# When the short block's first scores are computed, and where the gathers stand in a place

## The chip, the cores and the metric

The kernel runs on one core of a Trainium2 chip. The metric is the device time of one execution in microseconds (us). It is one program: an attention stage, and behind it a feed-forward stage. The change touches the attention stage alone.

## What is computed

Talking-heads attention over 8 images of 12 heads, 448 tokens and 64 channels, and then a feed-forward layer on its result:

```python
scores = scale * np.matmul(q, k.transpose(0, 1, 3, 2))
scores = np.einsum('bhij,hg->bgij', scores, w_pre)
scores = scores - np.max(scores, axis=-1, keepdims=True)
attn = np.exp(scores)
attn = attn / (np.sum(attn, axis=-1, keepdims=True) + 1e-09)
attn = np.einsum('bhij,hg->bgij', attn, w_post)
out = np.matmul(attn, v)
x = out.transpose(0, 2, 1, 3).reshape(B * S, H * D)
h = x @ w_in
y = (h - np.tanh(h)) @ w_out
```

## The kernel before

**Blocks, groups and places.** The 448 query tokens of an image `b` are cut into four chunks `m`: 120, 120, 120 and 88 tokens. A block is one chunk of one image (32 blocks, `i` = 4b + m); the short block is the one with m = 3. Heads are mixed with the 10 tokens x 12 heads of a group on the partitions, so each block is 12 groups (9 for the short one), 360 in all. Two groups are worked on together, in one pass of the main loop, which is called a place here; there are 180 places `p`, some 22 or 23 per image.

**What every place does.** TensorE (PE) multiplies the gathered scores of its two groups by `w_pre` (`premix`, L920). VectorE (DVE) takes the row maxima (`mx`, L929), ScalarE (ACT) the exponentials (L931), GpSimd (POOL) folds the sums into `w_post` (`norm`, `wr`, L940), and PE multiplies by that (`mix`, L957), for the place before. ACT copies the result to `at` at the start of the next place (L967).

**What some places do besides.** Each block also needs: its q transposed (`prep_q`, L842, from `qr`, loaded by `load_q`), its scores (`scores`, six head pairs, L876, copied out of PSUM by ACT and DVE in L881 to the tile `s`), and its values (`values`, two halves, L1000, copied by DVE in L1018). Each image also needs its keys transposed (`prep_k`, L816, copied to `kk` by L827 and L828). These jobs are dealt out to places by a planner ahead of the loop: `halved` lists for each job its earliest and its latest place, and the loop behind it gives each place the waiting job with the nearest latest place, one of the other kind (scores, `"s"`, or values, `"v"`) where that is possible. `prep_q` is put one place ahead of the first scores of its block, the `load_q` of the next block on the place of these scores, and `prep_k` where there is room. Two further planner steps spread single pairs over empty places. Every engine runs its instructions in the order in which they are written.

**Buffers around the change.** The scores of a block lie in `s` (tile pool `sp`, two buffers), token by token; `gather` (L909) is a DMA that moves the rows of one group from `s` to a tile `t` with the heads next to the tokens. So block i+1 writes where the last gathers of block i-1 read. In place p the two gathers for place p + 3 are issued. `ps_m` is a pool of four PSUM banks: a score pair takes two, a `prep_q`, `prep_k` or half of the values takes one each.

**SyncE's queue (SP).** All DMAs of this stage go through SyncE's queue, in order. Gathers are put there at once by `gather`. All other DMAs (loads of q, k and v, stores of `x`, and the DMAs of the weight conversion) are put on two lists, `queue` and `slow`, and `issue(6)` sends up to six of them in each place, those that were put there in an earlier place.

**The weight conversion.** In the background `Convert` splits the weights of the feed-forward layer in two parts and writes these and sums of them to DRAM (`cr` in, `wi`, `wo`, `ss`, `ts` out). `conv.step()` emits one phase of it per place on DVE (L81 and L82 in one phase, L90, L91 and L94 in another), ACT (L86, L99) and POOL (L84 to L129); `conv.more()` puts further loads on the list `slow`.

Of the kernel before, what the change touches and what calls it, by code (L numbers as in the profile page):

```python
# [148 lines left out]
def kernel_body(  # L149
# [74 lines left out]
    def open_early():  # L224
        ff.hid = pool("hid", 1, "left")
        ff.bias = pool("bias", 1, "left").tile([P, 2 * LINE], F32, name="bias", tag="bias")
        nc.gpsimd.memset(ff.bias[:, 0:1], GATE_A[1])
        nc.gpsimd.memset(ff.bias[:, 1:2], GATE_B[1])
        nc.gpsimd.memset(ff.bias[:, 2:3], -0.25)
        ff.xr, ff.xe, ff.xqa = pool("xr", 1, "left"), pool("xe", 1, "left"), pool("xqa", 1, "left")  # L230
        ff.plain = ctx.enter_context(ExitStack())
        ff.w0, ff.xp = pool("w0", 3, "left", ff.plain), pool("xp", NK, "left", ff.plain)

    def open_ps_h():
        ff.ps_h = ctx.enter_context(tc.tile_pool(name="ps_h", bufs=2, space=PSUM, side="left"))
# [501 lines left out]
    with ExitStack() as st:  # L737
# [32 lines left out]
        def issue(most):  # L770
            for x in (queue, slow):
                while x and most and x[0][0] < place[0]:
                    send(x, nc.sync)
                    most -= 1
# [131 lines left out]
        def gather(t, eng=nc.sync):  # L906
            i, g = groups[t]
            x = tq[t % RT]
            eng.dma_start(x[D - HP : D - HP + rows[t], :], sts[i][tokens[t].start : tokens[t].stop : tokens[t].step])  # L909
            tg[t] = x  # L910

        def premix(p):


            pss = [ps_p.tile([P, S], F32, name="ps_p", tag="ps_p") for _ in halves]
            ts = [tg.pop(2 * p + j) for j in range(2)]
            for j in (1, 0):
                for r in (1, 0):
                    k = slice(r * D, D + r * H * half_rows(2 * p + j)[r])
                    nc.tensor.matmul(pss[r][halves[j], :], wpre[k, :], ts[j][k, :], start=True, stop=True)  # L920
            return pss

        def expo(p, pss):
            zs = gp.tile([P, 3, 2], F32, name="zs", tag="zs")
            es = []
            for r, ps in enumerate(pss):

                mx = gp.tile([P, 1], F32, name="mx", tag="mx")
                nc.vector.tensor_reduce(out=mx, in_=ps, axis=AX.X, op=ALU.max, negate=True)  # L929
                e = gp.tile([P, S], F32, name="e", tag="e", bufs=4)  # L930
                nc.scalar.activation(e, ps, AF.Exp, bias=mx, scale=1.0, accum_out=zs[:, 0, r : r + 1])  # L931
                es.append(e)
            te[p] = [es, zs]

        def norm(p):
            zs = te[p][1]
            wr = gp.tile([P, 2, D], F32, name="wr", tag="wr", bufs=2)[:, :, :HP]
            nc.vector.tensor_scalar_add(zs[:, 1], zs[:, 0], 1e-9)
            nc.vector.reciprocal(zs[:, 2], zs[:, 1])  # L939
            nc.gpsimd.tensor_mul(  # L940
                wr, wpost[:, :HP].unsqueeze(1).to_broadcast([P, 2, HP]), zs[:, 2].unsqueeze(2).to_broadcast([P, 2, HP])
            )
            te[p].append(wr)

        def mix(p):

            es, _, wr = te.pop(p)
            ps = ps_o.tile([P, 2, 512], F32, name="ps_o", tag="ps_o")
            for j in range(2):
                i, g = groups[2 * p + j]  # L950
                if g == 0:
                    ats[i] = kp.tile([CP, NC, H, MT], F32, name="at", tag="at", bufs=2)
            for r, e in enumerate(es):
                for c in range(NC):
                    for j, a in enumerate(halves):
                        k = slice(a.start, a.start + H * half_rows(2 * p + j)[r])
                        nc.tensor.matmul(  # L957
                            ps[:CP, j, c * GP : (c + 1) * GP].rearrange("p (h i) -> p h i", i=GI)[:, :, r * GH : (r + 1) * GH],
                            e[k, c * CP : (c + 1) * CP], wr[k, r, :],
                            start=True, stop=True,  # L960
                        )

            def rest():
                (i0, _), (i1, _) = groups[2 * p], groups[2 * p + 1]
                n0, n1, at = rows[2 * p] // H, rows[2 * p + 1] // H, at_of[2 * p]
                if i0 == i1 and n0 == n1 == GI:
                    nc.scalar.copy(  # L967
                        ats[i0][:, :, :, at : at + 2 * GI].rearrange("p c h (j i) -> p j (c h) i", j=2),
                        ps[:CP, :, : NC * GP].rearrange("p j (x i) -> p j x i", i=GI),
                    )  # L970
                    return
                for j, (i, n) in enumerate(((i0, n0), (i1, n1))):
                    at = at_of[2 * p + j]
                    nc.scalar.copy(
                        ats[i][:, :, :, at : at + n],
                        ps[:CP, j, : NC * GP].rearrange("p (c h i) -> p c h i", c=NC, i=GI)[:, :, :, :n],
                    )

            return rest
# [102 lines left out]
        for w in range(2):  # L1082
            for at in AT[w]:
                x = repeat[:, w, at : at + HP].rearrange("p (i h) -> p i h", i=GH)
# [7 lines left out]
        for w in range(2):  # L1092
            for a in range(2):
                if w == 0:
                    x = both[:, w, a].rearrange("p (i g) -> p i g", i=GH)
                    of, step = ps_w[:, w, :].unsqueeze(1).to_broadcast([P, GH, H]), [[H, GH], [0, H]]
                else:
                    x = both[:, w, a].rearrange("p (g i) -> p g i", i=GH)
# [38 lines left out]
        NG = len(groups)  # L1137
# [16 lines left out]
        halved = []  # L1154
        for i in range(len(blocks)):

            f0, f1, f2 = first[i : i + 3]
            if i + 1 < len(blocks):
                lo = max(0, (f0 - 1) // 2 - 2)
                hi = f1 // 2 - 4  # L1160
                for x in range(0 if i else 1, 3):
                    e = lo + 2 * x if lo + 4 <= hi else lo + (hi - lo) * x // 2
                    halved.append((e if i else x - 1, hi, "s", i + 1, x))
            for x in range(2):
                halved.append(((f1 - 1) // 2 + 2, f2 // 2 + 1 if f2 < NG else NPL + 7, "v", i, x))
        at_s, at_v, p, kind = {}, {}, 0, None
        window = {i: (lo, hi) for lo, hi, k, i, _ in sorted(halved, reverse=True) if k == "s"}
        while halved:
            ready = sorted((x for x in halved if x[0] <= p), key=lambda x: (x[1], x[3:]))
            if ready:  # L1170
                x = ready[0]
# [3 lines left out]
                if x[2] == kind and other and x[1] > p + 1:  # L1175
                    x = other[0]
                halved.remove(x)
                _, _, kind, i, n = x
# [11 lines left out]
        def held(p):  # L1190
            return [a for f, *a in todo[p] if f is scores]

        for p in range(1, NPL):
            if any(f in (scores, values) for f, *a in todo[p]):
                continue
            for of, n in ((p - 1, 1), (p + 1, 0)):
                if len(held(of)) == 2 and window[held(of)[n][0]][0] <= p <= window[held(of)[n][0]][1]:
                    i, hp = held(of)[n]
# [4 lines left out]
        for i, (b, m) in enumerate(blocks):  # L1203
            p0 = first[i] // 2
            if i + 2 < len(blocks):
                p = at_s[i + 2, 0] - 1
# [8 lines left out]
        for b in range(1, B):  # L1215
            p, o, done = first[blocks.index((b - 1, 1))] // 2 - 5, 0, []
            for hq in range(3):
                if hq == 2:

                    p = max(p, done[0] + 1)  # L1220
# [41 lines left out]
        for p in range(NPL + 3):  # L1262
            if mixed:
                mixed()
                mixed = None
            if 2 <= p < NPL + 1:
                if p not in short:
                    conv.step()
                conv.more()
            place[0] += 1  # L1270
            for t in range(2 * p + 6 if p else 4, 2 * p + 8):
                if t < NG:
                    gather(t)
            issue(6)
            if p == NPL + 1:
                for f in start.pop(p):
                    f()
            if p < NPL:
                ps = premix(p)
            if 1 <= p < NPL + 1:  # L1280
                norm(p - 1)
            if p == NPL:
                for f in x0[1:]:
                    f()
            if p < NPL:
                expo(p, ps)
            if p > NPL:
                next(xq)
                next(xq)
            for f, *a in todo[p]:  # L1290
                f(*a)
            for f in sooner:
                f()
            sooner.clear()
            if 1 <= p < NPL + 1:
                mixed = mix(p - 1)
            for f in then + last:
                f()
            then.clear()
            last.clear()  # L1300
            if p == NPL - 3:
                conv.rest(now)
                early.close()
                open_early()
            if p == NPL - 1:
                early_ps.close()
                open_ps_h()
            for f in start.get(p, ()):
                f()
            for _ in range(pieces.get(p, 0)):  # L1310
                next(xl)
# [20 lines left out]
    late, left = None, 4 * NQ  # L1332
    for s in range(NS):
        more = s + 1 < NS
        for p in range(NQ):
# [16 lines left out]
            late = pair_step(s, p, late, share, between)  # L1352
# [16 lines left out]
        late = None  # L1369
# [33 lines left out]
```

## Time and profile before

| what | us |
|---|---|
| median of 3 timed runs | 1688.39 |
| their lowest and highest | 1685.31, 1690.20 |
| the profiled execution's own time | 1691.88 |
| its span, from the first to the last instruction | 1690.2 |
| PE busy | 1654.1 |
| DVE busy | 1235.9 |
| ACT busy | 1090.9 |
| POOL busy | 613.9 |

The profile shows one execution. Its lines name an engine, a line of the kernel, and what is written and read (`s<-ps_q` writes `s` from `ps_q`). In the lines of a timeline the first number is the start in the span, the second the duration, xN the number of instructions merged in the row, and the brackets at the end hold the engine's idle time just before and what ended it. In the lines by stretch come the stretch, its length, each engine's busy time in it (PE, weight loads, DVE, ACT, POOL) with the number of instructions, the granted share of PE's clock, the share of the DMA engines that was busy, and GB/s. The attention stage's places run from 25.92 us to some 834 us of the span.

### The profile page before, as it was taken

The page shows a single profiled execution, that of the slowest core. Times are in us where ns is not written, and L with a number is a line of the kernel's source. Part 1 is how long each engine was busy: PE and PEld are TensorE (multiplying, and loading weights), DVE is VectorE, ACT ScalarE, POOL GpSimd, SP SyncE. Part 2 cuts the span into 40 slices and gives each one's busy share as a digit, 9 for nine tenths or more (in the row PEclk, how much of TensorE's full clock was granted, in tenths as well). Part 3 has the DMA queues.
Part 4 walks back from the last instruction along what each step waited for, and adds up shares of the span by engine and source line. Part 5 has one row for each costly group of instructions (what it writes and reads, how often), then busy time and mean ns, then how long its engine had stood idle before and what let it go on. Part 6 is the DMA issues. An engine that isn't in the chain of part 4 may idle for free.

```text
span 1690.2 us, 40990 instructions
## 1 busy us (share of the span) xinstructions
PE 1654.1 (98%) x16068; PEld 1380.8 (82%) x16068; DVE 1235.9 (73%) x1939; ACT 1090.9 (65%) x1896; POOL 613.9 (36%) x824
## 2 busy tenths in 40 slices
PE   8999999999999999999999999999999999999999
PEld 6777777777777777777788888888888888889999
DVE  5777786877867777776497999868778868778422
ACT  4777776677767677776576776556667356666331
POOL 2577666767666677664100111201111101012100
PEclk9999999999999999999999999999999999999999
DMA  9878788798978979875778899989999989988993
GB/s 191 232 249 239 248 245 253 236 269 256 260 229 260 257 246 261 263 238 201 229 248 321 286 324 319 346 288 343 330 324 358 358 272 338 325 321 321 412 413 134
DMA packets 322672, 475.08 MB, mean 281 GB/s; under 512 B 105648, under 2 KB 255664, under 8 KB 322480
## 3 DMA queue, kind: packets, MB, share of 16 engines
q1 hardware_dynamic: 305660, 414.34, 76.7%
q0 software_dynamic: 16512, 57.68, 8.6%
q8 instruction: 128, 2.10, 0.5%
q14 instruction: 64, 0.52, 0.1%
q10 hardware_dynamic: 308, 0.43, 0.1%
HBM read 274.73 MB, written 120.59 MB: 234 GB/s over the span
## 4 chain that ended last, share of the span: by engine, by line
PE 84%; DVE 6%; DMA 4%; ACT 3%; issue 2%; POOL 1%; SPq 0%; DVEq 0%; ACTq 0%; POOLq 0%
PE ps_o L957 14%; PE ps_m L1000 8%; PE ps_p L920 8%; PE ps_h L289 7%; PE ps_h L292 7%; PE ps_h L290 7%; PE y L532 6%; PE ps_q L876 6%; PE y L530 6%; PE y L531 6%; PE ps_m L842 1%; DMA w<-wo 1%; DMA t<-s 1%; PE ps_m L816 1%; DVE mx L929 1%
## 5 line engine op out<-in xcount | busy, mean ns | idle before, releaser
L957 PEld LDWEIGHTS ps_o<-wr,e 60*112 60x112 f32 (+1 forms) x5760 | 304.0, 175 | 32.7 <-POOL wr L940 17.2
L957 PE MATMUL ps_o<-wr,e 60*112 60x60 f32 (+1 forms) x5760 | 313.0, 258 | 7.0 <-POOL wr L940 5.7
L931 ACT ACTIVATE e<-ps_p,mx 128x448 f32<-128x448 f32 x360 | 225.4, 632 | 110.9 <-DVE mx L929 55.8
L929 DVE TENSOR_REDUCE mx<-ps_p 128x1 f32<-128x448 f32 x360 | 206.6, 616 | 78.6 <-PE ps_p L920 78.1
L967 ACT COPY at<-ps_o 112x960 f32<-112x960 f32 x156 | 153.9, 987 | 104.1 <-PE ps_o L957 103.7
L920 PE MATMUL ps_p<-t,wpre 60*64 60x448 f32 (+1 forms) x1440 | 179.1, 565 | 1.6 <-DMA t<-s 1.6
L940 POOL TENSOR_TENSOR wr<-wpost,zs 128x120 f32<-128x120 f32 x180 | 69.9, 388 | 265.6 <-DVE zs L939 204.8
L1000 PEld LDWEIGHTS ps_m<-at,vr 112*64 112x64 f32 x3072 | 151.2, 139 | 18.5 <-issue 12.9
L1000 PE MATMUL ps_m<-at,vr 112*64 112x120 f32 (+1 forms) x3072 | 164.8, 265 | 0.0
L530 PE MATMUL y<-w,gh 128*128 128x384 f32 x440 | 148.4, 337 | 4.1 <-DMA w<-wo 3.0
L531 PE MATMUL y<-w,gh 128*128 128x384 f32 x440 | 147.6, 336 | 0.0
L532 PE MATMUL y<-w,gl 128*128 128x384 f32 x416 | 140.4, 337 | 2.5 <-DVE gl L448 2.5
L881 DVE COPY s<-ps_q 120x448 f32<-120x448 f32 (+1 forms) x192 | 112.3, 615 | 24.6 <-DMA t<-s 12.5
L876 PEld LDWEIGHTS ps_q<-kk,qh 64*120 64x120 f32 (+1 forms) x768 | 58.6, 173 | 85.2 <-issue 44.6
L876 PE MATMUL ps_q<-kk,qh 64*120 64x448 f32 (+1 forms) x768 | 121.6, 393 | 1.2 <-DVE kk L828 0.5
L881 ACT COPY s<-ps_q 120x448 f32<-120x448 f32 (+1 forms) x192 | 94.8, 535 | 19.9 <-DMA t<-s 9.6
L305 ACT ACTIVATE u<-h 128x1024 f32<-128x1024 f32 x56 | 59.6, 1064 | 72.0 <-DVE h L717 68.1
L645 POOL DMA_DIRECT2D gs<-ga x24 | 17.5, 730 | 242.5 <-DVE ga L328 242.5
L530 PEld LDWEIGHTS y<-w,gh 128*128 128x128 f32 x440 | 82.6, 188 | 9.0 <-issue 4.7
L531 PEld LDWEIGHTS y<-w,gh 128*128 128x128 f32 x440 | 82.6, 188 | 3.3
L442 ACT CAST gh<-gl 128x1024 fp32r<-128x1024 f32 x60 | 62.5, 1041 | 28.7 <-DMA gl<-gs 18.0
L532 PEld LDWEIGHTS y<-w,gl 128*128 128x128 f32 x416 | 78.0, 188 | 3.4 <-DVE gl L448 3.4
(372 smaller groups left out, 3955.6 us busy)
## 6 DMA issues: line engine op xcount, KB each, us to landing
t<-s SPq DMA_DIRECT2D x342, 210.0 KB
wa<-ss SPq DMA_DIRECT2D x96, 384.0 KB
gl<-gs SPq DMA_DIRECT2D x62, 512.0 KB
w<-wo SPq DMA_DIRECT2D x41, 768.0 KB
wa<-wi SPq DMA_DIRECT2D x72, 384.0 KB
w<-ts SPq DMA_DIRECT2D x36, 768.0 KB
gs<-gs POOLq DMA_DIRECT2D x24, 768.0 KB, 8.5
cr<-in_moe_w_in_dram SPq DMA_DIRECT2D x48, 256.0 KB
```

The source lines that it names most:

```text
L289: nc.tensor.matmul(ph, w[:, c, 0], xh, start=start and c == 0, stop=False, skip_group_check=True)
L530: nc.tensor.matmul(y, gh[:, tok], wh, start=first, stop=False, skip_group_check=True)
L531: nc.tensor.matmul(y, gh[:, tok], wl, start=False, stop=False, skip_group_check=True)
L532: nc.tensor.matmul(y, gl[:, tok], wh, start=False, stop=last, skip_group_check=True)
L876: nc.tensor.matmul(ps[:n, :S], qx[a, hp, :], kx[a, hp % 2], start=(x == 0), stop=(x == 2))
L881: eng(sts[i][:n, 2 * hp + j, :], ps[:n, :S])
L920: nc.tensor.matmul(pss[r][halves[j], :], wpre[k, :], ts[j][k, :], start=True, stop=True)
L929: nc.vector.tensor_reduce(out=mx, in_=ps, axis=AX.X, op=ALU.max, negate=True)
L931: nc.scalar.activation(e, ps, AF.Exp, bias=mx, scale=1.0, accum_out=zs[:, 0, r : r + 1])
L957: nc.tensor.matmul(ps[:CP, j, c * GP : (c + 1) * GP].rearrange("p (h i) -> p h i", i=GI)[:, :, r * GH : (r + 1) * GH], e[k, c * CP : (c + ...
L967: nc.scalar.copy(ats[i0][:, :, :, at : at + 2 * GI].rearrange("p c h (j i) -> p j (c h) i", j=2), ps[:CP, :, : NC * GP].rearrange("p j (x ...
L1000: nc.tensor.matmul(pv[j * D : (j + 1) * D, r, :n], vt[:, j, c, :], ats[i][:, c, 2 * hp + j, :n], start=(c == 0), stop=(c == NC - 1),)
```

## The change

It makes two edits in the part that is written once for all images:

```diff
                 for x in range(0 if i else 1, 3):
                     e = lo + 2 * x if lo + 4 <= hi else lo + (hi - lo) * x // 2
-                    halved.append((e if i else x - 1, hi, "s", i + 1, x))
+                    late = 1 if i % 4 == 2 and x == 0 else 0
+                    halved.append((e + late if i else x - 1, hi, "s", i + 1, x))
...
+            for t in range(2 * p + 6 if p else 4, 2 * p + 8):
+                if t < NG:
+                    gather(t)
             if 2 <= p < NPL + 1:
                 if p not in short:
                     conv.step()
                 conv.more()
             place[0] += 1
-            for t in range(2 * p + 6 if p else 4, 2 * p + 8):
-                if t < NG:
-                    gather(t)
             issue(6)
```

The first edit sets the earliest place of the first two score pairs (x = 0) of the block after chunk 2, which is the short block, one later. The planner then deals the jobs of four places of each image anew (of three in image 7, which has no keys to prepare for a next image). All other places keep their jobs. The second edit writes the two gathers of a place ahead of the conversion's step.

PE in image 2, at the first of these places (53): the half of the values that stood two places later, with the mix and premix of that place, now comes before the transposes of q.

```order
 L957 MATMUL ps_o<-wr,e 112x12x5 x16
 L920 MATMUL ps_p<-t,wpre 64x448 x4
+L1000 MATMUL ps_m<-at,vr 64x120 x24
+L957 MATMUL ps_o<-wr,e 112x12x5 x16
+L920 MATMUL ps_p<-t,wpre 64x448 x4
 L842 MATMUL ps_m<-ident,qr 128x88 x6
 L1000 MATMUL ps_m<-at,vr 64x120 x24
```

So place 53 holds values alone, and place 54 the q transposes and values. The two score pairs that were in place 54 are now in 55. PE in image 2, further on, where the k transposes (`kr`) stand:

```order
 L920 MATMUL ps_p<-t,wpre 64x448 x4
 L816 MATMUL ps_m<-ident,kr 128x112 x8
-L1000 MATMUL ps_m<-at,vr 64x120 x24
-L957 MATMUL ps_o<-wr,e 112x12x5 x16
-L920 MATMUL ps_p<-t,wpre 64x448 x4
 L876 MATMUL ps_q<-kk,qh 88x448 x4
 L876 MATMUL ps_q<-kk,ql 88x448 x2
```

The k transposes shared place 55 with values, and now share place 56 with a single score pair.

DVE in image 2 around the first score copies (`s<-ps_q`), before:

```order
L857 SCALAR_TENSOR_TENSOR ql<-ps_m,qh 128x3x88 x2
L1018 COPY x<-ps_m 128x3x12x10
L81 TENSOR_SCALAR cm<-cr 128x512
L82 TENSOR_SCALAR cr<-cr 128x512
L938 TENSOR_SCALAR zs<-zs 128x2
L939 RECIPROCAL zs<-zs 128x2
L929 TENSOR_REDUCE mx<-ps_p 128x1 x2
L881 COPY s<-ps_q 88x448 x2
```

and DVE at the same copies now, to the start of the next place:

```order
L857 SCALAR_TENSOR_TENSOR ql<-ps_m,qh 128x3x88 x2
L1018 COPY x<-ps_m 128x3x12x10
L938 TENSOR_SCALAR zs<-zs 128x2
L939 RECIPROCAL zs<-zs 128x2
L929 TENSOR_REDUCE mx<-ps_p 128x1 x2
L881 COPY s<-ps_q 88x448 x2
L90 TENSOR_SCALAR co<-cr 128x4x128
L91 SCALAR_TENSOR_TENSOR cr<-cm,co 128x512
L94 TENSOR_SCALAR co<-cr 128x4x128
```

The conversion's phases stay with their places, so that the copies now have another phase around them: L81 and L82 come a place before the one with the copies, and L90 to L94 a place after.

SyncE in image 2, from the gathers (`t<-s`) of places 54 and 55 on: only the load of q (`qr`) moves.

```order
 L909 DMA t<-s 120x1x448 x4
-L767 DMA qr<-in_q_dram 120x12x64
 L767 DMA ss_81<-ct 512x1x256
 L767 DMA cr<-in_moe_w_in_dram 128x2x256 x2
 L909 DMA t<-s 120x1x448 x2
+L767 DMA qr<-in_q_dram 120x12x64
 L767 DMA wi_69<-co 512x1x256
```

It now goes out behind a store, two loads and a pair of gathers. The gathers stand where they stood, in this image and in the others: the second edit alone leaves every engine's order as it was.

## The prediction

> **What bounds the kernel now.** I read the page first, then who waited for whom, then the timeline of TensorE's waits, then sums by stretch. On the page TensorE (PE) is busy for 98% of the span and holds 84% of the chain that ended last. So a change of order can win only where PE stands still or runs slowly, and can lose only by making it do so.
>
> ```profile
> span 1690.2 us, 40990 instructions
> PE 1654.1 (98%) x16068; PEld 1380.8 (82%) x16068; DVE 1235.9 (73%) x1939; ACT 1090.9 (65%) x1896; POOL 613.9 (36%) x824
> PE 84%; DVE 6%; DMA 4%; ACT 3%; issue 2%; POOL 1%; SPq 0%; DVEq 0%; ACTq 0%; POOLq 0%
> ```
>
> The waits (who, for what: us in total, times, longest) tell of a two-step chain in the attention stage. The key transposes (L816) wait for VectorE's score copies (L881), which free the PSUM bank that the transposes need; and these copies wait for DMAs that read `s`, the gathers.
>
> ```profile
> PEld ps_m L816 <- DVE s L881: 12.4, 6, 4.9
> PE ps_m L816 <- DVE s L881: 7.9, 4, 4.1
> DVE s L881 <- DMA t<-s: 12.5, 3, 6.0
> ```
>
> `s` has two buffers. The first score copy of block i+1 overwrites the rows that the last gather of block i-1 reads, so it waits until that gather has landed. In image 2 the timeline of SyncE, DVE and PE shows all of it:
>
> ```profile
> 259.15 0.98 PE L920 MATMUL ps_p<-t,wpre 60*64 60x448 f32 x8
> 261.31 3.50 SPq L767 DMA_DIRECT2D ss<-ct  x1
> 264.90 2.06 SPq L767 DMA_DIRECT2D cr<-in_moe_w_in_dram  x2
> 267.05 1.69 SPq L909 DMA_DIRECT2D t<-s  x2
> 273.22 1.15 DVE L881 COPY s<-ps_q 88x448 f32<-88x448 f32 x2 [6.03 <-DMA t<-s]
> 273.90 1.76 PE L816 MATMUL ps_m<-ident,kr 112*128 112x112 f32 x8 [4.10 <-DVE s L881]
> 275.59 4.40 PE L1000 MATMUL ps_m<-at,vr 112*64 112x120 f32 x48
> ```
>
> Place 53 begins at 259.15, but SyncE, behind a store that took 3.50 us to go out and two conversion loads, issues its two gathers only at 267.05 to 268.74. They have landed at 273.22, about 4.5 us after the issue's end. DVE has waited 6.03 us by then, and PE 4.10. The two PE groups after the wait are slow as well: beside them, rows of image 6, where the same work wasn't held up.
>
> ```profile
> 681.94 1.15 DVE L881 COPY s<-ps_q 88x448 f32<-88x448 f32 x2 [1.70 <-PE ps_o L957]
> 682.77 0.99 PE L816 MATMUL ps_m<-ident,kr 112*128 112x112 f32 x8
> 683.68 2.68 PE L1000 MATMUL ps_m<-at,vr 112*64 112x120 f32 x48
> ```
>
> The transposes took 1.76 instead of 0.99, the values 4.40 instead of 2.68. DVE's 1.70 us in image 6 is the same kind of wait (the engine named there was long done), and it reached no PE row.
>
> How often does this happen? Below are the four places of each image that the change reorders (in image 4 with one place more, where its delay ends): PE busy, the other engines, the granted clock, DMA.
>
> ```profile
> 57.00:76.04 19.04, 19.04 (x291) 15.02 (x289) 12.94 (x30) 13.54 (x32) 10.46 (x14) 1.00 0.90 230
> 157.96:179.89 21.93, 20.72 (x290) 16.48 (x288) 14.16 (x33) 13.16 (x31) 11.74 (x16) 0.92 0.92 238
> 259.15:284.93 25.78, 21.68 (x291) 17.29 (x289) 14.11 (x33) 13.39 (x31) 11.95 (x17) 0.87 0.94 269
> 367.33:386.37 19.04, 19.04 (x290) 15.02 (x289) 13.47 (x30) 13.51 (x31) 11.17 (x15) 1.00 0.84 255
> 465.92:492.29 26.37, 24.12 (x337) 17.90 (x335) 16.48 (x39) 16.35 (x37) 14.72 (x18) 0.94 0.81 242
> 570.68:592.85 22.17, 20.80 (x291) 16.41 (x289) 14.18 (x34) 13.42 (x31) 11.55 (x15) 0.92 0.92 259
> 672.19:691.22 19.03, 19.03 (x290) 15.01 (x289) 12.63 (x31) 13.60 (x32) 11.12 (x14) 1.00 0.91 253
> 386.37:389.58 3.21, 3.21 (x49) 2.33 (x47) 2.32 (x7) 2.63 (x7) 2.66 (x4) 1.00 1.02 338
> ```
>
> Undisturbed the four take 19.04 us at clock 1.00 (images 0, 3, 6). Images 1, 2 and 5 take 21.93, 25.78 and 22.17, which is 2.89, 6.74 and 3.13 too much. Image 4 takes 26.37 where 19.04 + 3.21 = 22.25 would do: 4.12 too much. Together 16.88 us. That is the whole stake, 1% of the span. PE's own idle time in it is 4.10 plus these:
>
> ```profile
> 169.82 1.70 PE L816 MATMUL ps_m<-ident,kr 112*128 112x112 f32 x8 [1.21 <-DVE s L881]
> 477.75 0.98 PE L816 MATMUL ps_m<-ident,kr 112*128 112x112 f32 x8 [1.18 <-DVE s L881]
> 485.82 1.88 PE L957 MATMUL ps_o<-wr,e 60*112 60x60 f32 x32 [1.08 <-POOL wr L940]
> 582.70 1.57 PE L816 MATMUL ps_m<-ident,kr 112*128 112x112 f32 x8 [1.38 <-DVE s L881]
> ```
>
> These make 1.21 + 4.10 + 1.18 + 1.08 + 1.38 = 8.95 us. The other 7.93 went to slower matmuls, in the very stretches whose granted clock is below 1.00.
>
> **The change, part by part.**
>
> *The gathers moved ahead of the conversion's step: nothing.* The gather goes to SyncE's queue at once, while the conversion's step only puts its own DMAs on lists, which `issue` sends later in the place. No engine's instructions change their order by it, and neither do their waits. I cost it at 0, with no cover needed.
>
> *The short block's first scores one place later.* In images 0 to 6 the places 8, 9, 10, 11 (53 to 56 in image 2) held: q transposes and values; two score pairs; k transposes and values; one score pair. They now hold: values; q transposes and values; two score pairs; k transposes and one pair. Each kind of place has a row in this trace:
>
> ```profile
> 220.52:225.76 5.24, 5.24 (x90) 4.31 (x88) 3.95 (x8) 2.44 (x6) 4.16 (x5) 1.00 0.92 265
> 367.33:373.17 5.84, 5.84 (x96) 4.82 (x94) 3.56 (x8) 3.67 (x9) 4.13 (x7) 1.00 0.79 221
> 373.17:377.00 3.83, 3.83 (x55) 2.79 (x53) 3.27 (x9) 3.60 (x8) 2.61 (x4) 1.00 0.90 295
> 247.54:251.70 4.16, 4.16 (x57) 3.18 (x55) 3.37 (x7) 2.92 (x7) 1.41 (x2) 1.00 0.85 253
> 251.70:255.29 3.59, 3.50 (x48) 2.32 (x47) 3.13 (x8) 3.24 (x8) 2.16 (x3) 1.00 0.92 241
> 461.50:465.92 4.42, 4.12 (x54) 2.88 (x52) 4.25 (x10) 3.40 (x9) 3.55 (x6) 1.00 0.98 326
> ```
>
> PE's work: 5.24 + 5.84 + 3.83 + 4.16 = 19.07 against 19.04, so +0.03 for each of 7 images, +0.2. In image 7 three places are permuted and nothing waits there: 0.
>
> What it removes: the two score pairs begin 5.24 + 5.84 = 11.08 us after the start of the place with the last gather, instead of 5.84, so 5.24 us later. The longest wait, 6.03, shrinks to about 0.8, the others go. A wait of 1.70 in image 6 reached no PE row, so 0.8 won't. I take all 16.88 us as gone, slow clock included, since it came only behind these waits. Bounds: 8.95 if the slow clock has another cause, 16.88 otherwise.
>
> What it adds on VectorE and ScalarE: k transposes and a score pair now share a 4.16 us place behind a place of two pairs, while the conversion's steps keep their places. The nearest rows: after such a place in image 2 (247.54) the next single-pair place took 3.59 instead of 3.21, and a two-pair place with a heavy conversion step (461.50) 4.42 instead of 3.83. So between 0 and 0.38 + 0.59 = 0.97 per image, 0 to 6.8 in all. A gain is possible only where other waits of such places shrink, and I see none tied to these. I take 0.4 per image, nearest to the 0.38 of the same combination: +2.8.
>
> The moved steps bring no DMA of their own but the q load: the second half of the values, now one place earlier, sends `x` out only for odd chunks, and here the chunk is 0; the k transposes and their copies to `kk`, one place later, are first read six places on. GpSimd's order stays.
>
> What it moves on SyncE: the load of q for the block after next is planned one place later and goes out behind one or more gathers and, in image 2, a store, two loads and a gather pair. There it stands behind this row:
>
> ```profile
> 279.08 1.65 SPq L909 DMA_DIRECT2D t<-s  x2
> 292.02 0.98 PE L920 MATMUL ps_p<-t,wpre 60*64 60x448 f32 x8
> 292.93 0.83 PE L842 MATMUL ps_m<-ident,qr 120*128 120x120 f32 x6
> ```
>
> Those gathers feed place 59, which began at 292.02 and would begin 6.74 us sooner, at 285.3. With the 4.5 us from above they land at 285.2. The q load, issued next (281.3), would land at 285.8, and its transposes would want it at 286.2. So in image 2 the cover is nearly used up; elsewhere PE comes forward by half as much. I price it at 0 to 3 us and take 0.5, as a shorter hold-up also lets SyncE's stores go earlier. This is what is late next.
>
> *Sum.* -16.88 + 0.2 + 2.8 + 0.5 = -13.4 us against the profiled execution's own 1691.88: 1678.5. That execution is 3.5 us above the timed median of 1688.39 and above all three timed runs. If it merely waited more, the timed result is 1678.5 too; if the 3.5 is on top of everything, 1688.39 - 13.4 = 1675.0. I take 1676.5.
>
> **The rivals.**
>
> *The new places cost PE more than the waits did (slower).* Place: the k transposes and score pair at place 11 and the pair behind them, whose PSUM banks VectorE must first free. For it: DVE was already 4.25 us busy in the 4.42 us place above. Against: the same combination at 247.54 ran at PE's pace. It decides from 16.88 / 7 = 2.4 us per image, and shows as slower from (16.88 + 5) / 7 = 3.1. In image 4, where a late wr and a slow clock followed the wait, one hold-up cost 4.12; at that in all seven the result is 1688.39 - 16.88 + 7 x 4.12 + 0.7 (the q load and PE's own work) = 1701.
>
> *The hold-up comes back (no change).* SyncE is late by its own stores and loads, and the waits let it catch up. Without them the gathers or q loads of the next block are late. For it: the 0.1 us of cover in image 2. Against: at 1, 4 and 5 the advance is 3 to 4 us. If half of 16.88 returns: 1688.39 - 8.4 + 3 = 1683 to 1687.
>
> *The slow clock is not the waits' doing.* Then only 8.95 of idle time goes: 1691.88 - 8.95 + 3.5 = 1686.4, or 1683 from the median. For it: the waits of 1.2 to 1.4 us are short. Against: every reordered stretch with a wait has a clock of 0.87 to 0.94, every one without has 1.00. The Trainium skill, "TensorE: Matmul & The Clock Gate" (HAM oscillation), says that the clock falls back after gaps above some 3.4 us; by that rule only image 2's 4.10 us could be the cause, and this rival would hold. The rows of images 1 and 5 speak against the rule, so I give it little.
>
> **How the numbers follow.** Some 0.3% (5 us) is what a measurement can tell from no change. Forecast (1670 to 1683): 0.79. Hold-up returns: 0.11, a fifth of it still below 1683.3. Slow clock stays: 0.04, half of it below. Slower: 0.06, of which some 0.04 above 1693.5. That makes faster 0.82, same 0.14, slower 0.04. The range runs from 1670 (all 16.88 from the median, less run spread) to 1686, which takes in the upper bounds of new waits and most of the returned hold-up.
>
> **What would show it.** Right: the eight stretches all near 19.1 to 19.6 us at clock 1.00, L816 no longer waiting for DVE's L881, gathers of image 2 still issued some 8 us into their place. Wrong: L842 or L920 waiting for a DMA around place 59, or a clock below 1.00 near the new place 11. The prediction falls if the timed runs hardly had these waits, or if each image gains a wait of 2 us elsewhere.

## The result, and the profile after

The changed kernel took 1681.34 us (median of ten runs, 1676.85 to 1685.17) beside 1688.82 for the one before (ten runs, 1685.31 to 1696.22): a ratio of 0.9946, with a 95% interval of 0.9931 to 0.9960. So it is 7.5 us faster. The forecast was 1676.5, with 1670 to 1686 as its range.

The profiled execution took 1681.62 us. First the lines of its page that answer to those shown of before (span, busy time of the engines, shares of the chain that ended last):

```profile
span 1679.8 us, 40980 instructions
PE 1652.0 (98%) x16068; PEld 1377.0 (82%) x16068; DVE 1244.1 (74%) x1939; ACT 1091.0 (65%) x1896; POOL 613.9 (37%) x824
PE 84%; DVE 6%; ACT 3%; DMA 3%; issue 2%; POOL 1%; SPq 0%; ACTq 0%; DVEq 0%; POOLq 0%
```

PE still carries the chain; its work is the same, and its span is 10.4 us shorter. Next the four reordered places of images 0 to 6, by stretch:

```profile
57.98:77.00 19.02, 19.02 (x291) 15.00 (x289) 12.20 (x28) 13.26 (x30) 10.24 (x14) 1.00 0.77 211
158.94:177.98 19.04, 19.04 (x290) 15.01 (x289) 14.49 (x31) 12.84 (x30) 11.75 (x16) 1.00 0.80 251
257.52:277.32 19.80, 19.37 (x290) 14.97 (x289) 14.29 (x30) 12.83 (x30) 12.40 (x17) 1.00 0.91 273
360.99:380.03 19.04, 19.04 (x291) 15.01 (x289) 12.20 (x29) 13.55 (x32) 11.33 (x15) 1.00 0.86 252
459.56:478.59 19.03, 19.03 (x290) 15.01 (x288) 14.48 (x31) 12.85 (x30) 11.64 (x15) 1.00 0.89 278
560.50:579.74 19.24, 19.24 (x290) 14.93 (x288) 14.62 (x31) 12.86 (x30) 12.23 (x15) 1.00 0.83 269
660.40:679.44 19.04, 19.04 (x290) 15.01 (x289) 12.21 (x30) 13.62 (x32) 11.19 (x14) 1.00 0.88 263
```

All seven stand between 19.02 and 19.80 us, at a granted clock of 1.00; four of them had taken 21.93 to 26.37 (the last with one place more, 22.25 undisturbed), at 0.87 to 0.94. Among the waits, no row of L816 for VectorE's L881 is left. The timeline of image 2 shows why:

```profile
257.52 0.98 PE L920 MATMUL ps_p<-t,wpre 60*64 60x448 f32 x8
259.31 4.19 SPq L767 DMA_DIRECT2D ss<-ct  x1
265.63 1.68 SPq L909 DMA_DIRECT2D t<-s  x2
271.61 1.15 DVE L881 COPY s<-ps_q 88x448 f32<-88x448 f32 x2 [0.59 <-PE ps_q L876]
273.54 0.99 PE L816 MATMUL ps_m<-ident,kr 112*128 112x112 f32 x8
```

The gathers are as late as before: issued 8.1 us into the place that begins at 257.52, behind a store that took 4.19 to go out. The score copy starts at 271.61, 14.09 us into that place, and it had started 14.07 us into it before (273.22 - 259.15): it is no later and no earlier. What is new is that PE and VectorE had other work until shortly before it. The row puts VectorE's 0.59 us of idle time down to PE's scores, but these had ended at 271.17, and the trace has the last landing that the copy waits for at 271.33, 0.28 us ahead of it; before, that landing was at 272.95 and the copy 0.27 us later. So the copy still waits for the gathers, some 0.6 us instead of 6.03, and that no longer reaches PE. The transposes take 0.99.

What the change cost shows as PE's waits for `wr` in the places that now hold the k transposes beside a score pair, and in those behind them:

```profile
275.61 1.78 PE L957 MATMUL ps_o<-wr,e 60*112 60x60 f32 x32 [0.30 <-POOL wr L940]
279.45 1.78 PE L957 MATMUL ps_o<-wr,e 60*112 60x60 f32 x32 [0.31 <-POOL wr L940]
284.02 1.78 PE L957 MATMUL ps_o<-wr,e 60*112 60x60 f32 x32 [0.48 <-POOL wr L940]
```

### The profile page after: what moved, and what is told of

Same layout as the page of the kernel before. It is cut to its first block, busy times and chain, and to the rows that moved or that the text cites. A ratio compares the mean times of both kernels' runs of the same rounds, so it can differ in the third digit from the quotient of the medians.

```text
span 1679.8 us, 40980 instructions
## 1 busy us (share of the span) xinstructions
PE 1652.0 (98%) x16068; PEld 1377.0 (82%) x16068; DVE 1244.1 (74%) x1939; ACT 1091.0 (65%) x1896; POOL 613.9 (37%) x824
## 4 chain that ended last, share of the span: by engine, by line
PE 84%; DVE 6%; ACT 3%; DMA 3%; issue 2%; POOL 1%; SPq 0%; ACTq 0%; DVEq 0%; POOLq 0%
PE ps_o L957 14%; PE ps_m L1000 8%; PE ps_p L920 8%; PE ps_h L289 7%; PE ps_h L292 7%; PE ps_h L290 7%; PE y L530 7%; PE y L532 7%; PE y L531 6%; PE ps_q L876 6%; PE ps_m L842 1%; ACT e L931 1%; DVE mx L929 1%; PE y L502 1%; PE y L501 1%
## 5 line engine op out<-in xcount | busy, mean ns | idle before, releaser
L920 PE MATMUL ps_p<-t,wpre 60*64 60x448 f32 (+1 forms) x1440 | 179.5, 566 | 1.8 <-DMA t<-s 1.7
L1000 PEld LDWEIGHTS ps_m<-at,vr 112*64 112x64 f32 x3072 | 147.6, 137 | 22.0 <-issue 14.1
L1000 PE MATMUL ps_m<-at,vr 112*64 112x120 f32 (+1 forms) x3072 | 161.1, 261 | 0.0
L881 DVE COPY s<-ps_q 120x448 f32<-120x448 f32 (+1 forms) x192 | 112.4, 615 | 7.9 <-PE ps_q L876 7.6
L881 ACT COPY s<-ps_q 120x448 f32<-120x448 f32 (+1 forms) x192 | 94.8, 536 | 6.9 <-PE ps_q L876 6.7
```

The source lines that it names most:

```text
L881: eng(sts[i][:n, 2 * hp + j, :], ps[:n, :S])
L1000: nc.tensor.matmul(pv[j * D : (j + 1) * D, r, :n], vt[:, j, c, :], ats[i][:, c, 2 * hp + j, :n], start=(c == 0), stop=(c == NC - 1),)
```

## The experiments

Three theories stand in the expectations. W: the gain is the hold-up removed, the waits of the score copies for the last gathers with the slow clock behind them. G: the second edit brings it, gathers that go out first. R: the new mixture of jobs in the places helps by itself. Each short diff is against the kernel before; where it says "changed kernel", the edit is made on that. Ratios are to the kernel before on the same chip, with 95% intervals.

**The second edit alone.**

```diff
+            for t in range(2 * p + 6 if p else 4, 2 * p + 8):
+                if t < NG:
+                    gather(t)
             if 2 <= p < NPL + 1:
...
-            for t in range(2 * p + 6 if p else 4, 2 * p + 8):
-                if t < NG:
-                    gather(t)
             issue(6)
```

> The second edit alone (gathers ahead of the conversion's step), planner as before. Theory W (the gain is the score copies' wait for gathers, and its slow clock): no engine's order moves, so the same time as before within 0.2%, and in the profile images 1, 2, 4 and 5 (or others, as the DMAs fall) again take 2 to 7 us more than 19.04 in the four places. Rival G (gathers that go out first are what helps): 0.3 to 0.5% faster, and the last gathers of the place go out sooner after its start than 8 us in image 2.

1690.53 us (12 runs), ratio 1.0010, 0.9995 to 1.0026. So this edit moves nothing, and G falls. Its profile holds a second sample of the hold-ups, in images 1, 2, 4 and 5 (four places each):

```profile
158.90:179.81 20.91, 19.36 (x291) 14.94 (x289) 14.31 (x34) 13.40 (x31) 11.72 (x16) 1.00 0.89 254
259.00:284.50 25.50, 21.11 (x294) 16.72 (x292) 14.11 (x33) 13.40 (x31) 11.91 (x17) 0.87 0.90 262
465.60:487.37 21.77, 19.37 (x294) 14.94 (x292) 14.28 (x34) 13.43 (x31) 11.58 (x15) 1.00 0.86 256
569.10:588.27 19.17, 19.17 (x292) 14.93 (x290) 14.19 (x35) 13.53 (x31) 11.56 (x15) 1.00 0.90 274
```

Against 19.04 these are 1.87 + 6.46 + 2.73 + 0.13 = 11.2 us, with the same instruction order for which the first profile showed 16.88. Only image 2 lost clock. PE's idle time in these places (the length less PE's busy time) is 1.55 + 4.39 + 2.40 = 8.34, about as much as the 8.95 of the first profile; what differs is the rest, the slower matmuls: 2.85 here, 7.93 there.

**The first edit alone.**

```diff
-                    halved.append((e if i else x - 1, hi, "s", i + 1, x))
+                    late = 1 if i % 4 == 2 and x == 0 else 0
+                    halved.append((e + late if i else x - 1, hi, "s", i + 1, x))
```

> The first edit alone (short block's first scores one place later), gathers where they stood. Theory W: all of the change's effect, 0.4 to 0.7% faster than before, L816 no longer waiting for DVE's score copies. Rival G: no more than a part of it, under 0.2%.

1683.79 us (8 runs), ratio 0.9963, 0.9947 to 0.9979: faster, and its interval overlaps that of the whole change. The gain is the first edit's. In its profile no L816 waits for L881, but the gathers of image 2 are late here too: the score copy waits 1.2 us for them, and PE's premix 0.71 us in the same places, which took 20.73.

**The delay at another block** (changed kernel).

```diff
-                    late = 1 if i % 4 == 2 and x == 0 else 0
+                    late = 1 if i % 4 == 3 and x == 0 else 0
```

> The same delay of one place for another block: the first scores after chunk 3 (chunk 0 of the next image) instead of those after chunk 2. There the profile of before shows no wait of the score copies. Theory W: the waits at the short block stay and nothing is removed, so between no change and 0.3% slower (0 to 1 us per image for the new mixture). Rival R: faster by 0.2% or more, as by the change.

1691.80 us (12 runs), ratio 1.0016, 1.0001 to 1.0031. The delay now moves scores of the next image's first block. The hold-ups of the short block are there as before; images 1 and 2:

```profile
162.90:183.71 20.81, 19.36 (x292) 14.93 (x288) 14.29 (x34) 13.45 (x31) 11.78 (x16) 1.00 0.87 252
263.70:289.13 25.43, 22.31 (x292) 17.81 (x288) 14.10 (x33) 13.52 (x31) 11.96 (x17) 0.87 0.93 269
```

A delay as such gains nothing; it must be that of the short block.

**The delay only where the profile showed a hold-up, and only where it showed none** (changed kernel; blocks 6, 10, 18, 22 are images 1, 2, 4, 5, and blocks 2, 14, 26, 30 are images 0, 3, 6, 7).

```diff
-                    late = 1 if i % 4 == 2 and x == 0 else 0
+                    late = 1 if i in (6, 10, 18, 22) and x == 0 else 0
```

> The change's first edit only in images 1, 2, 4 and 5, those in which the score copies held PE up; images 0, 3, 6 and 7 keep the old places. Theory W: the whole gain of the change, 0.4 to 0.6% below before, and the four places at 19 to 21 us in every image. Rival R (the mixture of places helps by itself, in all images alike): about half of it.

```diff
-                    late = 1 if i % 4 == 2 and x == 0 else 0
+                    late = 1 if i in (2, 14, 26, 30) and x == 0 else 0
```

> The first edit only in images 0, 3, 6 and 7, where no wait reached PE. Theory W: within 0.2% of before, the waits of images 1, 2, 4 or 5 still there (22 to 26 us in their four places). Rival R: the other half of the gain, 0.2 to 0.3%.

The first took 1681.88 us (12 runs), ratio 0.9961, 0.9944 to 0.9978; the second 1690.75 (12 runs), ratio 1.0001, 0.9985 to 1.0018. Within the intervals all of the gain lies in the four images with hold-ups. R had put 0.2 to 0.3% into images 0, 3, 6 and 7, which lies outside the second interval, and falls. By stretch, images 1, 2, 4 and 5 with the delay there:

```profile
159.50:178.53 19.03, 19.03 (x290) 15.01 (x288) 14.47 (x31) 12.83 (x30) 11.76 (x16) 1.00 0.88 258
258.10:278.04 19.94, 19.29 (x293) 14.93 (x291) 14.09 (x30) 12.97 (x30) 12.20 (x17) 1.00 0.91 276
460.20:479.22 19.02, 19.02 (x292) 15.01 (x288) 14.47 (x31) 12.80 (x30) 11.72 (x15) 1.00 0.87 264
561.30:580.54 19.24, 19.24 (x294) 14.92 (x292) 14.56 (x31) 12.84 (x30) 12.25 (x15) 1.00 0.92 279
```

and the same images with the delay elsewhere (image 4 with the place where its hold-up ends):

```profile
158.00:179.56 21.56, 19.36 (x291) 14.93 (x288) 14.29 (x34) 13.42 (x31) 11.75 (x16) 1.00 0.92 247
258.80:285.20 26.40, 21.87 (x290) 17.52 (x288) 14.07 (x33) 13.35 (x31) 11.95 (x17) 0.87 0.89 271
466.20:492.81 26.61, 24.12 (x337) 17.90 (x335) 16.48 (x39) 16.25 (x37) 14.89 (x19) 0.94 0.80 239
571.50:592.23 20.73, 19.36 (x292) 14.93 (x288) 14.10 (x35) 13.58 (x31) 11.55 (x15) 1.00 0.91 260
```

The waits go with the order of these places: they are gone in the first kernel, and in the second PE is idle for 2.20, 4.53, 2.49 and 1.37 us. The clock below 1.00 is gone in the first too, but in the second only images 2 and 4 have it: images 1 and 5 waited at 1.00.

**Making the gathers earlier instead of the copies later.** Here the planner is that of before; the gathers of chunk 1's last two groups go to ScalarE's queue.

```diff
+            two = [t for t in range(2 * p + 6 if p else 4, 2 * p + 8) if t < NG]
+            ends = p and any(groups[t][0] % 4 == 1 and groups[t][1] == 11 for t in two)
...
-                    gather(t)
+                gather(t, nc.scalar if ends else nc.sync)
```

> The planner as before, so the scores at their old place; but the last two gathers of each chunk 1 (seven or eight places in all) are put on ScalarE's DMA queue instead of SyncE's. Theory W: they no longer stand behind SyncE's stores and loads, land before the score copies want them, and the waits of L816 go: 0.4 to 0.9% faster, at least as much as the change, since the places keep their old mixture; some 1.7 us more on ScalarE in each of these places is hidden (ACT busy 3.7 of 5.8 us). Rival R (the new mixture of the places is what helps PE, not the wait): no faster than before, or slower by ScalarE's time.

1700.65 us (7 runs), ratio 1.0074, 1.0047 to 1.0101: slower, and W's expectation of the time missed. The timeline of image 2 shows the rest:

```profile
263.45 3.46 ACTq L909 DMA_DIRECT2D t<-s  x2
267.04 0.63 ACT L931 ACTIVATE e<-ps_p,mx 128x448 f32<-128x448 f32 x1 [6.67 <-DMA t<-s]
267.82 2.38 PE L920 MATMUL ps_p<-t,wpre 60*64 60x448 f32 x8 [3.22 <-ACT e L931]
275.71 0.98 PE L816 MATMUL ps_m<-ident,kr 112*128 112x112 f32 x8
```

L816 no longer waits for L881, as W says. But ScalarE did nothing else for 6.67 us: some 3.1 us ahead of the issue, which by the trace ended when earlier gathers had landed (263.37), and 3.46 us for the issue of two gathers, where 1.7 had been expected. Its exponentials were late, and PE waited 3.22 us for them. So the issue of these gathers held a wait of its own, for gathers ahead of them, and here it stopped the engine that had to compute. Whether SyncE's issues hold the same wait isn't shown.

**Holding the conversion's DMAs back** (planner of before; in the place of chunk 1's last gathers and the two ahead of it, the conversion's list isn't sent).

```diff
+        ends = {(t - 6) // 2 for t, (i, g) in enumerate(groups) if i % 4 == 1 and g == ngs[1] - 1}
+        holds = {p - x for p in ends for x in range(3)}
...
-            issue(6)
+            issue(6, (queue,) if p in holds else None)
```

> The kernel before, but in the place of the last gathers of chunk 1 and in the two places ahead of it issue(6) leaves the conversion's DMAs (list slow) on their list. Theory W, with SyncE held up by the conversion's stores and loads as its cause: the last gathers go out within 3 us of their place's start, the score copies no longer wait, L816 neither, and with the places as they were: 0.3 to 0.9% faster. If instead the transfers of q, k, v and x hold the gathers up: the waits stay and the time is within 0.2%. A cost is possible where held loads come late for the conversion, whose phases then move to other places.

1688.64 us (12 runs), ratio 0.9993, 0.9977 to 1.0009. So the expected gain of 0.3 to 0.9% did not come. PE's waits at L816 fell to 0.2 us, but the held store was now late for the conversion's step on VectorE, and PE waited for `wr` behind it, in image 1 for 1.93 us:

```profile
171.84 0.43 DVE L90 TENSOR_SCALAR co<-cr 128x512 int32<-128x512 int32 x1 [2.51 <-DMA wi<-co]
174.39 3.21 PE L957 MATMUL ps_o<-wr,e 60*112 60x60 f32 x32 [1.93 <-POOL wr L940]
```

The wait removed came back as another. In image 2 a merged row of four gathers still took 6.63 us to issue without those DMAs ahead, so they aren't the only cause:

```profile
263.11 6.63 SPq L909 DMA_DIRECT2D t<-s  x4
```

**Making the gathers later,** behind `issue(6)`: first with the planner of before, then in the changed kernel.

```diff
+            issue(6)
             for t in range(2 * p + 6 if p else 4, 2 * p + 8):
                 if t < NG:
                     gather(t)
-            issue(6)
```

> The kernel before, with the two gathers of each place written behind the up to six DMAs that issue(6) sends, so that every gather goes out later on SyncE. Theory W: the last gathers of chunk 1 land still later, the score copies and L816 wait in more images and longer: 0.3 to 1.5% slower, with the four places of images 1, 2, 4 and 5 above the 20 to 26 us of before, and slow clock behind them. Rival R (the mixture of places is what counts, the waits are harmless): within 0.2% of before.

> The changed planner with the gathers of each place behind issue(6). Theory W: the later scores leave 5.2 us more for the landing, so most of the lateness is taken up: 0.1 to 0.6% faster than before, and at least 0.4% faster than the same gathers with the old planner. Rival R: as far below the old planner's version as the change is below before, and neither moved by the gathers' place.

1706.48 us (6 runs), ratio 1.0102, 1.0081 to 1.0122; and 1707.59 (6 runs), ratio 1.0099, 1.0074 to 1.0124. W had expected the first to be slower through L816 and the second to be still faster. Both are slower, and for another reason: the gathers now miss the premix that reads them. In the first:

```profile
PE ps_p L920 <- DMA t<-s: 12.3, 6, 3.8
PE ps_m L816 <- DVE s L881: 2.4, 2, 2.0
```

In the second, L920 waits 12.2 us, also six times, and L816 not at all; image 2's four places took 19.23. The order after gives slack to the score copies but none to the premix. R missed as well: it expected the two kernels to stand apart by the change's gain, and they measure alike. The pair says nothing on the size of W's stake.

**Taking the change's own cost away** (changed kernel): no step of the conversion in any place with k transposes and one score pair, then only in two such places (56 and 124, images 2 and 5).

```diff
+        crowd = {p for p in range(9, NPL - 20) if sorted(f.__name__ for f in work_of[p]) == ["prep_k", "prep_k", "scores"]}
...
-                if p not in short:
+                if p not in short and p not in crowd:
```

> The changed kernel, with the conversion's step left out in the places that hold k transposes and a single score pair (the new place 11 of each image and some like it). In the profile after the change VectorE's chain (two-pair copies, conversion phase, maxima, k copies) is late there in images 2 and 5, and PE waits for wr in the three places from there, 0.3 to 0.5 us each. Theory: 1 to 4 us less than the change, 0.5 to 0.7% below before. If the conversion's phases fall on worse places elsewhere: no better than the change.

```diff
-                if p not in short:
+                if p not in short and p not in (56, 124):
```

> The change, with the conversion's step left out in places 56 and 124 alone (images 2 and 5, where VectorE's heavy phase met k transposes and a score pair). The ten or so skips of the earlier run pushed the conversion's last steps into the end of the stage; two should not. Theory: 1 to 3 us below the change in the stage, 0.45 to 0.65% below before; if the shift by one or two places costs as much elsewhere, no better than the change.

1683.78 us (12 runs), ratio 0.9976, 0.9959 to 0.9994; and 1680.78 (8 runs), ratio 0.9953, 0.9937 to 0.9970. In the first the four places took 19.02 to 19.04 in images 0 to 6, so the waits for `wr` there are the conversion step's doing. But the skipped steps are made up at the end of the stage, where POOL was busy 35.45 us in 60, against 10.60 in the changed kernel (the second row):

```profile
770.00:830.00 60.00, 54.64 (x778) 42.13 (x777) 36.26 (x78) 38.46 (x83) 35.45 (x48) 0.94 0.67 225
```

```profile
770.00:830.00 60.00, 58.06 (x824) 44.45 (x820) 30.21 (x68) 35.66 (x82) 10.60 (x20) 0.97 0.59 199
```

The second version measures the same as the change. Its two skips moved the later phases by a place or two: the four places of images 2 and 5 took 19.04, but those of image 4 19.28, and the two places behind took some 3.84 and 4.55 us in images 4 and 6, as those of images 2 and 5 had. The price moved to other images, the second case of its expectation. Neither version clearly beat the change.

## Why the prediction was right, and which sizes were off

The places of the attention stage, from the first to the start of the last, before and after:

```profile
25.92:828.67 802.75, 789.35 (x11557) 609.75 (x11557) 593.84 (x1319) 576.47 (x1299) 508.58 (x637) 0.99 0.83 245
```

```profile
25.31:817.43 792.12, 785.27 (x11556) 604.16 (x11556) 601.11 (x1319) 576.66 (x1299) 508.80 (x637) 1.00 0.82 248
```

They are 10.63 us shorter, and what lies ahead of them and behind them changed by -0.61 and +0.84: together the 10.4 of the span. Term by term:

- **The gathers' edit, 0.** Right: 1.0010, with an interval around 1.
- **The waits removed, 16.88, slow clock included.** Right as a mechanism: in the profiled execution all of it is gone, the clock of these stretches with it, and images 1, 2, 4 and 5 carry the gain. The size was that of one execution. The second edit's profile had 11.2, and the rows of the delay in images 0, 3, 6 and 7 have 2.52 + 7.36 + (26.61 - 22.25) + 1.69 = 15.9. PE's idle time makes up 8.95, 8.34 and 10.59 of these three; the slow clock's part is what swings, 7.93, 2.85 and 5.3. The prediction booked that part in full, since slow clock came only behind these waits; but it doesn't come behind each of them. The measured gain and the 4.8 of the next term make some 7.5 + 4.8 = 12.3 for the median run, an estimate. The timed runs show the clock's part as well: the mean granted clock was 0.9967 in the ten of the changed kernel, and 0.9933 to 0.9939 in the three sets of 23 to 26 runs of the kernel before that stand beside the experiments. That is some 0.003 of 1689 us, so some 5 us of clock, by estimate.
- **VectorE in the new places, +2.8 within 0 to 6.8.** Too small: it cost 4.8. Of that, 0.76 and 0.20 lie in the four places of images 2 and 5, and the rest behind them. In images 2 and 5 the two places behind took 8.41 together, where 7.09 and 7.08 stood before (after, then before):

```profile
277.32:285.73 8.41, 7.62 (x100) 5.07 (x99) 8.23 (x16) 6.22 (x16) 5.94 (x7) 1.00 0.90 251
579.74:588.15 8.41, 7.63 (x101) 5.07 (x99) 8.22 (x16) 6.28 (x17) 5.93 (x7) 1.00 0.72 220
```

```profile
284.93:292.02 7.09, 7.09 (x101) 5.03 (x99) 6.19 (x14) 5.40 (x14) 6.28 (x7) 1.00 0.47 176
592.85:599.93 7.08, 7.08 (x101) 5.03 (x99) 6.18 (x14) 5.46 (x15) 6.27 (x7) 1.00 0.67 240
```

VectorE's busy time there went from 6.19 to 8.23 us of 8.41. Its timeline in image 2 after, from the conversion's phase of place 56 on:

```profile
272.87 0.55 DVE L90 TENSOR_SCALAR co<-cr 128x512 int32<-128x512 int32 x1
277.44 1.16 DVE L828 TENSOR_TENSOR kk<-ps_m,kk 128x448 fp32r<-128x448 f32 x2 [0.84 <-ACT kk L827]
280.37 1.33 DVE L81 TENSOR_SCALAR cm<-cr 128x512 f32<-128x512 f32 x1
281.62 1.53 DVE L82 TENSOR_SCALAR cr<-cr 128x512 int32<-128x512 int32 x1
```

The copies of k (L828) now lie in the first of these two places, behind the phase L90 to L94 that had followed them: the two instructions more. L81 and L82, which had taken 0.41 and 0.43, take 1.33 and 1.53 there; what stretched them isn't shown. Without the conversion's step in places like 56 (the first of the two versions above) the two places behind took 3.22 and 4.17 in image 2, 7.39 together, and 3.22 and 3.83 in image 5. Images 1, 4 and 6 add 0.34, 0.33 and 0.53, and images 0 and 3 nothing, where the forecast spread 0.4 evenly: the price lay where the conversion's phase met the copies of k.

- **The q load, +0.5.** It cost nothing: it went out at 277.52 in image 2, not at the estimated 281.3, and neither L842 nor L920 waited there.
- **What no term covered, +1.54.** A wait that is in both profiles brought a slow stretch in the one after (last section). It belongs to the execution, not to the change.

So -16.88 + 4.8 + 1.54 = -10.5 against -10.63 measured in the profiles. The forecast of 1676.5 lies 4.8 us below the median of 1681.34. Two terms were mis-sized: the costs on VectorE, by 1.3 in the sum (4.8 against 2.8 + 0.2 + 0.5), and the stake, which was 16.88 in the profiled execution and some 12.3 in the median run, by the estimate above. The sum took off half of the 3.5 us between that execution and the median. But two executions of the same engine order differ by 5.7 us in these hold-ups alone (16.88 and 11.2), more than the 3.5; so the 1678.5 made against the profiled execution's own time was the better figure.

Of the rivals, "the hold-up comes back" didn't happen in the changed kernel, but something like it became of both attempts to get the gathers out earlier (ScalarE's queue, the conversion held back): a wait came back at another engine. "The new places cost more" had the right place and, at 4.8 in all against the 16.88 it needed, too small a price. "The slow clock is not the waits' doing" is wrong in the main: with the waits gone, these places run at 1.00 in every image, in the change and in the first edit alone. But the argument against it, that every stretch with a wait is slow, did not hold in other profiles: images 1 and 4 of the second edit, and images 1 and 5 of the kernel with the delay in images 0, 3, 6 and 7, had 1.37 to 2.40 us of idle time at 1.00. The last section shows how far a wait decides the clock. Which transfers the late gathers wait for isn't settled: the conversion's are a part, and a third buffer of `s` wasn't tried.

## What to carry to other kernels

When a short instruction waits for a DMA that frees its buffer, writing the instruction later, among work that has to be done anyway, can remove the harm where moving the DMA only moves the wait: here the copy starts as late as before, but the engines behind it are busy meanwhile, and the two attempts on the DMAs' side (another queue, other DMAs held back) gained nothing. A wait that shows in one profile must be sized over several executions before it is booked as a gain, above all where slow clock comes with it; a background job that keeps its places while the foreground moves must be laid against the new places one by one.

## What the runs showed of the hardware

PE's granted clock fell in whole stretches of about 3.4 us (3.41, 6.83 or 10.24 in the records), and waits of PE far shorter than that could bring one on, though not each time. PE's wait for `wr` in place 6 is in both profiles, 1.28 us before and 1.29 after:

```profile
51.44 1.78 PE L957 MATMUL ps_o<-wr,e 60*112 60x60 f32 x32 [1.28 <-POOL wr L940]
53.15:57.00 3.85, 3.85 (x55) 2.94 (x53) 3.78 (x9) 2.80 (x8) 2.77 (x3) 1.00 0.81 217
```

```profile
50.87 1.78 PE L957 MATMUL ps_o<-wr,e 60*112 60x60 f32 x32 [1.29 <-POOL wr L940]
52.59:57.98 5.39, 5.39 (x55) 3.66 (x53) 4.09 (x9) 3.26 (x8) 3.10 (x4) 0.69 0.90 231
```

The place behind it ran at 1.00 before and at 0.69 after, which cost 1.54 us. Of ten profiles with this wait (1.27 to 1.29 us), five show the fall and five don't.

The clock records of the traces tell the two apart. Within each of the thirteen traces, all slow stretches start whole multiples of 3.413 us apart, on a grid that lies differently in the span of each execution. Where 1.20 us or more of this wait falls into one window of the grid, the next window runs at half clock (five profiles); where the grid splits the wait, so that no window holds more than 1.11 us of it, the clock stays (five). After the change the wait, 49.58 to 50.87, lies whole in the window 49.12 to 52.53, and the clock is 0.50 from there to 55.95; before, a window's edge at 50.47 splits it. So the same wait is punished in one execution and not in the next. This boundary holds for this place alone: in image 4 of the second edit's profile a window with 1.34 us of idle time brought no fall, so idle time isn't all that counts.

The Trainium skill, "TensorE: Matmul & The Clock Gate" (Part 1), gives the clock a free-running window of some 3.4 us: the traces agree with it, by the grid of 3.413 us. Its rule that PE should have no idle gaps above about 3.4 us (HAM oscillation) doesn't agree: 1.3 us brought the clock down, in half of the cases.

This is one source of the spread between executions of the same kernel: of the 24 runs of the kernel before that stand beside the last experiments, the fastest, 1681.97 us, had a mean clock of 0.998, and the slowest, 1698.47 us, 0.990.
